# Backward of a memory-attention segment loop: order of the dS turns, the dK and dV products, and the row folds

## The chip, the cores and the metric

The kernel runs on one core of a Trainium2 chip. The metric is device time in microseconds (us) of one execution, from the first to the last instruction. Before the change it is 3257.82 us, the median of 3 runs (3256.99 to 3260.57).

## What is computed

The reference is one layer and its gradients: a layer norm with a modulation, an attention with recurrent memory, a second layer norm and a gated feed-forward part. The kernel returns the output and the gradients for x, the first memory, Wq, Wk, Wv, Wo, the three feed-forward weights, c and w_mod. What matters here is the attention and its gradient. The sequence of 2048 rows is cut into 64 segments of 32 rows; each segment has 8 memory rows in front, which are the first 8 output rows of the segment before it:

```python
mem = mem0
for s in range(n_seg):                      # 64 segments
    h = jnp.concatenate([mem, xs], axis=1)  # 8 + 32 rows
    q, k, v = (jnp.einsum('btd,dhe->bhte', h, W) for W in (Wq, Wk, Wv))   # 32 heads of 128
    scores = jnp.einsum('bhqe,bhke->bhqk', q, k) * scale
    p = _softmax(jnp.where(mask[None, None], scores, -1e9), axis=-1)
    o = jnp.einsum('bhqk,bhke->bhqe', p, v)
    o = jnp.einsum('bhte,hed->btd', o, Wo)
    mem = o[:, :M, :].copy()
    outs.append(o[:, M:, :])
```

The backward pass goes through the segments from the last to the first. The gradient of a segment's memory rows goes into the segment before it, so the 64 steps depend on each other.

## The kernel before, in words

The program has phases: the forward loop over segments (phase2), the feed-forward part with its gradients (phase3), the backward loop over segments (phase4) and the weight gradients (phase5). The change touches phase4 and two helpers which phase2 uses too.

**Tiling of a backward step.** The 32 heads of a segment are packed three to a group of 120 rows, 11 groups in all. The groups are handled in three parts of 4, 4 and 3 groups (`NP`, `PG`), because a PSUM tile holds 4 groups of 128 columns. A step of the loop at L1384 does this, in program order:

- `col_pass` (L1464) multiplies the incoming gradient by Wo; the two halves are copied out as `RAd`, one by VectorE and one by ScalarE. `turn` (L1469) transposes them into `dOT`.
- `dp`, `prod` and `ds` (L1472 to L1484) form dS: TensorE accumulates `dp_ps`, VectorE multiplies it by the stored probabilities (L1425).
- `grad_mm("dVT", ...)` gives dV in three parts (`gv0` to `gv2`), `grad_mm("dKT", ...)` gives dK (`gk0` to `gk2`) and `grad_part("dQT", ...)` gives dQ. Each part is a PSUM tile `g_ps` (L1436), which `grad_out` copies to SBUF through `evac` (L61 is ScalarE, L63 VectorE).
- dQ needs dS transposed. `dstt(pi)` (L1448) makes a part of it: TensorE transposes into a PSUM tile `tps` (L1352), and ScalarE copies that into `dST`.
- `dht` (L1455) multiplies dV, dK and dQ by the transposed weights, 96 narrow matmuls (L211) which accumulate in one PSUM tile, `dh_ps`. Four column groups of it have to be added up: `fold_split` (L271) writes a high and a low bf16 part of the tile (`dh_hi` by ScalarE, L278; `dh_lo` by VectorE, L282), and `fold_sum` (L286) adds the groups by matmuls with a selection matrix, into `dh_ft`. ScalarE copies the memory rows of that to `dyT_next` (L1523), with which the next step begins.
- `store_rows` (L295) casts `dh_ft` to bf16 on VectorE (`dh_tb`, L299) and appends a function to the list `self.later`. `pop_later` takes one function from that list and runs it: it transposes, copies (`dh_rb`, L305) and stores the rows from GpSimd (L306).

**The tail block.** The last 8 rows of each segment are collected over four segments (`TailRows`) and multiplied by the weights as one block, a quarter of its 96 matmuls per step (`chunk`), into a PSUM tile `dh_tps`. When the fourth quarter is done, `split` runs `fold_split` on that tile (`dh_b_hi`, `dh_b_lo`), and appends the sum (`dh_b_ft`) to `self.later`. Both uses of `fold_split` share their SBUF buffers by tag.

**What sets the order.** `pin` (L251) chains each engine's instructions of the loop in the order in which they are written. So the order of the calls in the loop is the order on every engine: an instruction that waits holds up all that stands behind it on its engine.

**PSUM.** `psp` has 6 buffers which all tiles with the tag "p" share in turn (`pass_ps`, `turn_ps`, `g_ps`, `dp_ps`, `tps`, `dh_ft` and so on), and `psb` has one each for `dh_ps` and `dh_tps`. A tile with the tag "p" can be written only when the tile six before it has been copied out.

**Transfers.** SyncE issues, in this order per step: the DMA transposes that turn dVT, dKT and dQT into rows (`rows_x`, L1444, three buffers in turn), the loads of `Qst` and `Kst` for the next step (L1357; one buffer each, so a load waits for the products that read the old content), and the loads of the stored forward tiles (L1340, L1343). GpSimd issues the stores of `rows_x` (L1446), by `store_rows_x`, in the next step, and small copies of tail rows into `dOst` (L1372).

Of the kernel before, what the change touches and what calls it, by code (L numbers as in the profile page):

```python
# [7 lines left out]
BF16 = mybir.dt.bfloat16  # L8
# [11 lines left out]
class Cfg:  # L20
    def __init__(self, NS=64, phases=("p0", "p1", "p2", "p3", "p4", "p5")):
        self.S_full = 2048
        self.D = 512
        self.DC = 4
        self.H = 32
        self.E = 128
        self.T = 32
        self.M = 8
        self.L = 40
        self.F = 1792  # L30
        self.FC = 14
        self.NS = NS
        self.S = NS * self.T
        self.NT = self.S // 128
        self.G = 11
        self.XW = 33 * 40 + 8
        self.scale = self.E ** -0.5
        self.phases = phases


class K:
# [226 lines left out]
                self.tc.add_manual_dep(ins, last[ins.engine].name, mybir.DependencyInfo(  # L268
                    mybir.DependencyClass.NoSync, mybir.DependencyReason.DATA), reason="program order")

    def fold_split(self, pool, ps, name):  # L271

        nc = self.nc
        parts = []
        for h in range(2):
            sl = slice(256 * h, 256 * h + 256)
            hi = pool.tile([128, 256], BF16, name=name + "_hi", tag=f"hi{h}", bufs=1)
            nc.scalar.activation(hi[:], ps[:, sl], AF.Copy)  # L278
            parts.append(hi)
        for h in range(2):  # L280
            lo = pool.tile([128, 256], BF16, name=name + "_lo", tag=f"lo{h}", bufs=1)
            nc.vector.tensor_tensor(lo[:], ps[:, 256 * h:256 * h + 256], parts[h][:], op=ALU.subtract)  # L282
            parts.append(lo)
        return parts
# [951 lines left out]
    def phase4(self):  # L1236
# [7 lines left out]
        with self.p4_ctx as ctx:  # L1244
            WqT, WkT, WvT, WoT, negones = self.WqT, self.WkT, self.WvT, self.WoT, self.negones
# [4 lines left out]
            sb2 = ctx.enter_context(tc.tile_pool(name="p4s2", bufs=2, reuse_waits="tile"))  # L1250
            psp = ctx.enter_context(tc.tile_pool(name="p4ps", bufs=6, space=PSUM, reuse_waits="tile"))
            psb = ctx.enter_context(tc.tile_pool(name="p4psb", bufs=1, space=PSUM, reuse_waits="tile"))
            NP = 3
# [28 lines left out]
            def part3(t, pi):  # L1282
                return t[:, pi * PW:min((pi + 1) * PW, G * GW)].rearrange("p (g x) -> p g x", x=GW)
# [71 lines left out]
            def load_rows(t, dram, s):  # L1355
                if s >= 0:
                    nc.sync.dma_start(gl3(t)[0:120, :, :], dram[s, 0:120, :, :])  # L1357
# [16 lines left out]
            dO_tails(NS - 1)  # L1374
            nseg_t = 128 // T
            row_stores = []

            def store_rows_x(left):
                while len(row_stores) > left:
                    row_stores.pop(0)()  # L1380
# [3 lines left out]
            for s in reversed(range(NS)):  # L1384
# [43 lines left out]
                def grad_part(nm, lh, rh, xt, pi, eng):  # L1428
                    grad_out(nm, xt, pi, eng, grad_mm(nm, lh, rh, pi))

                def grad_mm(nm, lh, rh, pi):
                    ps = ps_f32("g_ps")
                    n = min(PG, G - pi * PG)
                    for j in range(n):
                        g = pi * PG + j
                        nc.tensor.matmul(ps[:, j, :], lhsT=lh[:, g * GW:(g + 1) * GW], rhs=rh[:, g * GW:(g + 1) * GW],  # L1436
                                         start=True, stop=True)
                    return ps

                def grad_out(nm, xt, pi, eng, ps):  # L1440
                    self.evac(eng, part3(xt, pi), ps[:, 0:min(PG, G - pi * PG), :])
                    if pi == NP - 1:
                        rows = rxp.tile([128, G, 128], BF16, name="rows_x")
                        nc.sync.dma_start(rows[:], xt[:, :], transpose=True)  # L1444
                        dram = {"dVT": self.DVR, "dKT": self.DKR, "dQT": self.DQR}[nm][s]
                        row_stores.append(lambda: nc.gpsimd.dma_start(dram, rows[:]))  # L1446

                def dstt(pi):  # L1448
                    ps = transposes_part(dS, pi)
                    self.evac("act", part3(dST, pi), ps)  # L1450

                dh_ps = [None]
                n_dh = [0]
# [1 line left out]
                def dht(X, WT, pi):  # L1455
                    if dh_ps[0] is None:
                        dh_ps[0] = psb.tile([128, 512], F32, name="dh_ps", tag="dh")
                    for h in range(pi * PG * 3, min(H, (pi + 1) * PG * 3)):
                        off = (h // 3) * GW + (h % 3) * 32
                        self.col_mm(dh_ps[0], X[:, off:off + 32], WT[:, h, :], n_dh[0], 3 * H)  # L1460
                        n_dh[0] += 1

                for hf in range(2):
                    self.col_pass(psp, WoT, hf, lambda c: dyT[:, c, :], RAd, ("dve", "act")[hf])  # L1464
                    nc.gpsimd.tensor_copy(dOst[0:96, 512 * hf:512 * hf + 512], RAd[0:96, 512 * hf:512 * hf + 512])  # L1465
                store_rows_x(1)
                if s == 0:
                    self.p5_first()
# [23 lines left out]
                store_rows_x(0)  # L1492
                if s == 0:
                    self.p5_second()
                gv2 = grad_mm("dVT", dOst, Pst, 2)
                dstt(0)
                gk0 = grad_mm("dKT", Qst, dS, 0)
                dstt(1)
                gk1 = grad_mm("dKT", Qst, dS, 1)
                grad_out("dKT", dKT, 0, "dve", gk0)  # L1500
                grad_out("dVT", dVT, 2, "act", gv2)
                dstt(2)
                gk2 = grad_mm("dKT", Qst, dS, 2)
                load_rows(Qst_t, self.QST, s - 1)
                if s > 0:
                    dO_tails(s - 1)
                grad_out("dKT", dKT, 1, "dve", gk1)
                grad_out("dKT", dKT, 2, "dve", gk2)
                self.pop_later()
                for pi in range(NP):  # L1510
                    grad_part("dQT", Kst, dST, dQT, pi, "act")
                load_rows(Kst_t, self.KST, s - 1)
                dht(dVT, WvT, 2)
                for pi in range(NP):
                    dht(dKT, WkT, pi)
                for pi in range(NP):
                    dht(dQT, WqT, pi)
                parts = self.fold_split(sb2, dh_ps[0], "dh")
# [2 lines left out]
                ft = self.fold_sum(psp, parts, "dh", "p")  # L1521
                if dyT_next is not None:
                    nc.scalar.activation(dyT_next[:, :, 0:M], ft[:, :, 0:M], AF.Copy)  # L1523
                tail.split()
                if s > 3:
                    if s4 >= 2:
                        proj_b(s // 4 - 1, 3 - s4)()
# [2 lines left out]
                then = None  # L1530
# [4 lines left out]
                        for c in range(DC):  # L1535
                            nc.sync.dma_start(dm[:, c * 128:(c + 1) * 128], rb[32 * c:32 * c + M, :])

                self.store_rows(psp, sb2, ft, self.DHA[s], "dh", "p", then)
                if s4 == 0:
                    tail.begin(s, [WvT, WkT, WqT])  # L1540
            store_rows_x(0)
            self.pin(i0)
            tail.finish()
# [258 lines left out]
class TailRows:  # L1802

    def __init__(self, k, pool, psp, psb, n, name, dram_b, npieces=4):
        self.k, self.pool, self.psp, self.psb, self.n, self.name = k, pool, psp, psb, n, name
        self.dram_b, self.npieces = dram_b, npieces
        self.cur = None
        self.pieces = []  # L1810
        self.whole = None
# [10 lines left out]
    def begin(self, s0, ws):  # L1822
        while self.pieces:
            self.chunk()
        self.split()
        cfg, H = self.k.cfg, self.k.cfg.H
        tiles, self.cur = self.cur, None
        order = [(i, h) for i in range(self.n) for h in range(H)]
        per = len(order) // self.npieces
        st = {}  # L1830

        def piece(u):
            def f():
                if u == 0:
                    st["ps"] = self.psb.tile([128, 512], F32, name=f"{self.name}_tps", tag="b")
                for n in range(u * per, (u + 1) * per):
                    i, h = order[n]
                    self.k.col_mm(st["ps"], tiles[i][:, h, :], ws[i][:, h, :], n, len(order))
                if u == self.npieces - 1:
                    self.whole = st["ps"], s0  # L1840
            return f

        self.pieces = [piece(u) for u in range(self.npieces)]
# [4 lines left out]

    def split(self):
        if self.whole is None:  # L1850
            return
        (ps, s0), self.whole = self.whole, None
        parts = self.k.fold_split(self.pool, ps, self.name + "_b")

        def summed():
            ft = self.k.fold_sum(self.psp, parts, self.name + "_b", "p")
            self.k.store_rows(self.psp, self.pool, ft, self.dram_b[s0 // 4], self.name + "_b", "p")

        self.k.later.append(summed)

    def finish(self):
        while self.pieces:
            self.chunk()
        self.split()
        while self.k.later:
            self.k.pop_later()
# [85 lines left out]
```

## Time and profile before

The profile is of one execution of 3260.3 us. Busy times and shares are of the whole span.

| engine | busy us | share | instructions |
|---|---|---|---|
| TensorE (PE) | 3003.8 | 92% | 38650 |
| weight loads (PEld) | 1718.3 | 53% | 38650 |
| VectorE (DVE) | 1562.7 | 48% | 4106 |
| ScalarE (ACT) | 1225.3 | 38% | 2906 |
| GpSimd (POOL) | 1431.2 | 44% | 3037 |

The backward loop runs from about 1631 to 2655 us. In the stretch from 2000 to 2400 us TensorE is busy for 382.48 of 400 us, VectorE for 190.54, ScalarE for 187.11; the DMA engines move 257 GB/s.

In the rows of the views, L61 or L63 is a line of a helper, so a group is known by the tile that it writes and the tile that it reads (`dST<-tps`). "Idle before" gives how long the engine stood still ahead of an instruction, and what ended that. A busy TensorE isn't TensorE at its peak: matmuls overlap, and their ends are modelled. The chain of work follows the program back from its last instruction, at each step to what released it, so that it shows which of several waits ended last.

### The profile page before, as it was taken

What the parts mean: (1) busy time and instruction counts of PE and PEld (TensorE: products, weight loads), DVE (VectorE), ACT (ScalarE), POOL (GpSimd) and SP (SyncE); (2) the same over time, 40 slices, a digit from 0 to 9 for tenths busy, and PEclk for the clock granted to TensorE, in tenths of its full rate; (3) what the DMA queues carried; (4) which work ended last, traced back from release to release, by engine and by line L of the source; (5) the groups of instructions that cost most, each with busy time, mean ns of one, the idle gap of its engine ahead of it and who ended that gap; (6) DMA issues with size and microseconds to landing.
All of it is one profiled execution on the core that took longest, in us unless ns stands there. A gap on an engine that the chain in (4) does not pass through costs nothing.

```text
span 3260.3 us, 96121 instructions
## 1 busy us (share of the span) xinstructions
PE 3003.8 (92%) x38650; PEld 1718.3 (53%) x38650; DVE 1562.7 (48%) x4106; ACT 1225.3 (38%) x2906; POOL 1431.2 (44%) x3037
## 2 busy tenths in 40 slices
PE   6999999999998799988989999999999979999999
PEld 3555555555555444445555555555555544454454
DVE  5655655666655777633244444444444431322321
ACT  3555555555554333312144444444444420100111
POOL 3555555655555466520244444444444431333322
PEclk8999999999999899999999999999999999999999
DMA  8565555555566898897589999999999999998886
GB/s 295 175 172 169 172 170 167 169 166 171 169 165 181 212 216 214 204 270 227 187 223 251 252 253 257 259 258 265 254 256 245 252 238 219 240 209 191 198 229 162
DMA packets 862018, 699.40 MB, mean 215 GB/s; under 512 B 560690, under 2 KB 734274, under 8 KB 861444
## 3 DMA queue, kind: packets, MB, share of 16 engines
q1 hardware_dynamic: 737220, 483.44, 62.9%
q0 software_dynamic: 52912, 147.43, 13.2%
q10 hardware_dynamic: 71440, 62.40, 7.6%
q8 instruction: 304, 4.98, 0.7%
q14 instruction: 142, 1.16, 0.1%
HBM read 293.60 MB, written 275.02 MB: 174 GB/s over the span
## 4 chain that ended last, share of the span: by engine, by line
PE 43%; DMA 8%; ACT 2%; issue 2%; DVE 1%; POOL 1%; SPq 1%; ACTq 0%; DVEq 0%; POOLq 0%
PE dh_ps L211 10%; PE gps L1746 9%; PE pass_ps L222 4%; PE g_ps L1436 4%; PE gps5o L1759 3%; PE gps L1146 3%; PE dh_tps L211 3%; DMA rows<-DKR 2%; DMA Kst<-KST 2%; DMA rows<-OSR 1%; PE dp_ps L1415 1%; ACT RAd L61 1%; PE tps L1352 1%; PE dp_ps L1423 1%; PE dh_ft L291 1%
## 5 line engine op out<-in xcount | busy, mean ns | idle before, releaser
L1746 PE MATMUL gps<-rows,hrows 128*128 128x512 bf16 (+2 forms) x2160 | 419.5, 357 | 4.8 <-DVE ot L63 4.3
L1746 PEld LDWEIGHTS <-hrows 128*128 128x128 bf16 x2160 | 211.6, 98 | 211.0 <-issue 7.3
L222 PEld LDWEIGHTS <-hT 128*32 128x32 bf16 x6144 | 158.7, 97 | 177.5 <-ACT hT L785 24.5
L1465 POOL COPY dOst<-RAd 96x512 bf16<-96x512 bf16 x128 | 77.5, 612 | 376.1 <-DVE RAd L63 367.1
L282 DVE TENSOR_TENSOR dh_lo<-dh_ps,dh_hi 128x256 bf16<-128x256 f32 x128 | 48.4, 420 | 322.5 <-ACT dh_hi L278 322.5
L1750 POOL DMA_DIRECT2D out_dram<-ot x108 | 81.2, 754 | 235.5 <-DVE ot L63 141.1
L792 POOL TENSOR_TENSOR Pst<-Pst,rden 120x1408 bf16<-120x1408 bf16 x63 | 159.4, 2531 | 18.5 <-issue 7.7
L63 DVE CAST ot<-gps 128x512 bf16<-128x512 f32 (+3 forms) x76 | 47.8, 632 | 248.6 <-DMA out_dram<-ot 117.9
L1759 PE MATMUL gps5o<-WoT,rows 128*128 128x512 bf16 x600 | 131.8, 382 | 24.1 <-DMA rows<-OSR 24.1
L61 ACT ACTIVATE ot<-gps 128x512 bf16<-128x512 f32 (+3 forms) x75 | 41.1, 548 | 282.8 <-DMA out_dram<-ot 111.5
L306 POOL DMA_DIRECT2D AOA<-at_rb x64 | 36.7, 574 | 248.8 <-DVE at_rb L305 135.4
L61 ACT ACTIVATE dST<-tps 128x512 bf16<-128x512 bf16 (+1 forms) x192 | 102.2, 567 | 105.5 <-PE tps L1352 105.5
L222 PE MATMUL pass_ps<-Wv,hT 128*32 128x512 bf16 x2048 | 122.2, 381 | 18.0 <-ACT hT L785 18.0
L63 DVE CAST dKT<-g_ps 128x512 bf16<-128x512 f32 (+1 forms) x192 | 112.2, 640 | 50.3 <-issue 44.2
L694 DVE TENSOR_TENSOR Ost<-or_ps,rden 120x512 bf16<-120x512 f32 (+1 forms) x192 | 124.3, 647 | 23.1 <-PE or_ps L692 1.2
L211 PE MATMUL dh_ps<-WvT,dVT 128*32 128x512 bf16 x2048 | 134.9, 384 | 0.0
L1425 DVE SCALAR_TENSOR_TENSOR dS<-dp_ps,Pst_l 128x512 bf16<-128x512 f32 (+1 forms) x192 | 112.2, 640 | 32.2 <-PE dp_ps L1423 32.1
L222 PE MATMUL pass_ps<-WoT,dyT 128*32 128x512 bf16 x2048 | 122.5, 381 | 5.1 <-ACT dyT L1523 5.1
L211 PE MATMUL at_ps<-Wo,OT 128*32 128x512 bf16 x2048 | 122.3, 381 | 0.0
L211 PE MATMUL dh_ps<-WkT,dKT 128*32 128x512 bf16 x2048 | 121.7, 379 | 0.0
L211 PE MATMUL dh_ps<-WqT,dQT 128*32 128x512 bf16 x2048 | 121.7, 379 | 0.0
L222 PE MATMUL pass_ps<-Wk,hT 128*32 128x512 bf16 x2048 | 121.6, 379 | 0.0
(409 smaller groups left out, 7231.1 us busy)
## 6 DMA issues: line engine op xcount, KB each, us to landing
OSR<-Ost SPq DMA_DIRECT2D x64, 352.0 KB
OT<-OT SPq DMA_DIRECT2D x64, 352.0 KB
PS<-Pst SPq DMA_DIRECT2D x64, 352.0 KB
OT_l<-OT SPq DMA_DIRECT2D x64, 352.0 KB
Pst_l<-PS SPq DMA_DIRECT2D x64, 352.0 KB
DVR<-rows_x POOLq DMA_DIRECT2D x64, 352.0 KB, 5.5
DKR<-rows_x POOLq DMA_DIRECT2D x64, 352.0 KB, 7.2
DQR<-rows_x POOLq DMA_DIRECT2D x64, 352.0 KB, 5.4
```

Of the source, the lines that this page charges most:

```text
L61: return nc.scalar.activation(out, in_, AF.Copy)
L63: return nc.vector.tensor_copy(out, in_)
L211: self.nc.tensor.matmul(ps[32 * j:32 * j + 32, :], lhsT=lhsT, rhs=w, start=(n < 4), stop=(n >= total - 4), tile_position=(0, 32 * j))
L222: self.nc.tensor.matmul(ps[32 * j:32 * j + 32, :], lhsT=lhs(c), rhs=rhs, start=(c == 0), stop=(c == DC - 1), tile_position=(0, 32 * j))
L694: nc.vector.tensor_tensor(part3(Ost, pi)[0:120, 0:n, :], or_ps[0:120, 0:n, :], rden[:, pi * PG:pi * PG + n].unsqueeze(2).to_broadcast([120 ...
L792: nc.gpsimd.tensor_tensor(Pst[0:120, :, :], Pst[0:120, :, :], rden[:, :].unsqueeze(2).to_broadcast([120, G, 128]), op=ALU.mult)
L1146: nc.tensor.matmul(ps[:], lhsT=h2r[:, j, c * 128:(c + 1) * 128], rhs=xr[:, j, :], start=(j == 0), stop=(j == NT - 1))
L1425: nc.vector.scalar_tensor_tensor(out=part3(dS, pi), in0=ps[:, 0:n, :], scalar=cfg.scale, in1=part3(Pst, pi), op0=ALU.mult, op1=ALU.mult)
L1436: nc.tensor.matmul(ps[:, j, :], lhsT=lh[:, g * GW:(g + 1) * GW], rhs=rh[:, g * GW:(g + 1) * GW], start=True, stop=True)
L1746: nc.tensor.matmul(ps[:, 0:ng * E], lhsT=hrows[:, tp_, c * 128:(c + 1) * 128], rhs=rows[:, tp_, 0:ng * E], start=(tp_ == 0), stop=(tp_ == ...
L1750: nc.gpsimd.dma_start(outw[c * 128:(c + 1) * 128, h0:h0 + 3 * (ng - 1) + 1:3, :], ot[:, 0:ng * E].rearrange("p (h e) -> p h e", e=E))
L1759: nc.tensor.matmul(pss[gg][:], lhsT=rows[:, tp_, gg * E:(gg + 1) * E], rhs=dyrows[:, tp_, :], start=(tp_ == order[0]), stop=(tp_ == order[ ...
```

## The change

The loop body is put in another order, one copy goes to another engine, and two helpers run later.

- All three `dstt` (the turns of dS) stand ahead of the three dK products. The third dV product (`gv2`), which stood ahead of them all, goes behind dK. The aim is that dST is ready when dQ wants it.
- The copy of the middle part of dST is made by VectorE instead of ScalarE, and the copy-out of `gv2` stands behind both remaining ones on ScalarE.
- The load of `Qst` is issued ahead of the copies of dK, and dK's DMA transpose comes ahead of dV's.
- In `dht`, dK comes ahead of the third part of dV.
- The tail block's `split` moves from the end of the step in which its fourth quarter was computed into the next step, between dQ and `dht`; its sum is run by a `pop_later` after dK and dV of `dht`. `begin` doesn't split any more, `finish` does so first.
- `store_rows`, with its cast `dh_tb`, is put off to the next step, behind `col_pass`.
- `fold_split` and `TailRows` get a `tags` argument with the default "", which nothing sets.

```diff
                 def dstt(pi):
                     ps = transposes_part(dS, pi)
-                    self.evac("act", part3(dST, pi), ps)
+                    self.evac("dve" if pi == 1 else "act", part3(dST, pi), ps)
...
+                if pend:
+                    pend.pop()()
                 store_rows_x(1)
...
+                for pi in range(NP):
+                    dstt(pi)
+                gks = [grad_mm("dKT", Qst, dS, pi) for pi in range(NP)]
+                load_rows(Qst_t, self.QST, s - 1)
                 gv2 = grad_mm("dVT", dOst, Pst, 2)
-                dstt(0)
-                gk0 = grad_mm("dKT", Qst, dS, 0)
-                dstt(1)
-                gk1 = grad_mm("dKT", Qst, dS, 1)
-                grad_out("dKT", dKT, 0, "dve", gk0)
-                grad_out("dVT", dVT, 2, "act", gv2)
-                dstt(2)
-                gk2 = grad_mm("dKT", Qst, dS, 2)
-                load_rows(Qst_t, self.QST, s - 1)
                 if s > 0:
                     dO_tails(s - 1)
-                grad_out("dKT", dKT, 1, "dve", gk1)
-                grad_out("dKT", dKT, 2, "dve", gk2)
+                for pi in range(NP):
+                    grad_out("dKT", dKT, pi, "dve", gks[pi])
+                grad_out("dVT", dVT, 2, "act", gv2)
                 self.pop_later()
                 for pi in range(NP):
                     grad_part("dQT", Kst, dST, dQT, pi, "act")
+                split = tail.split()
                 load_rows(Kst_t, self.KST, s - 1)
-                dht(dVT, WvT, 2)
                 for pi in range(NP):
                     dht(dKT, WkT, pi)
+                dht(dVT, WvT, 2)
+                if split:
+                    self.pop_later()
                 for pi in range(NP):
                     dht(dQT, WqT, pi)
                 parts = self.fold_split(sb2, dh_ps[0], "dh")
...
-                tail.split()
...
-                self.store_rows(psp, sb2, ft, self.DHA[s], "dh", "p", then)
+                pend.append(lambda ft=ft, s=s, then=then: self.store_rows(psp, sb2, ft, self.DHA[s], "dh", "p", then))
                 if s4 == 0:
                     tail.begin(s, [WvT, WkT, WqT])
+            pend.pop()()
             store_rows_x(0)
...
     def begin(self, s0, ws):
         while self.pieces:
             self.chunk()
-        self.split()
...
     def split(self):
         if self.whole is None:
-            return
+            return False
...
     def finish(self):
+        self.split()
         while self.pieces:
             self.chunk()
         self.split()
```

More of the change, by code (lines that the diff above doesn't have):

```diff
@@ L269, in pin_behind, with fold_split @@
                     mybir.DependencyClass.NoSync, mybir.DependencyReason.DATA), reason="program order")
-    def fold_split(self, pool, ps, name):
+    def fold_split(self, pool, ps, name, tags=""):
         nc = self.nc
@@ L276, in fold_split @@
             sl = slice(256 * h, 256 * h + 256)
-            hi = pool.tile([128, 256], BF16, name=name + "_hi", tag=f"hi{h}", bufs=1)
+            hi = pool.tile([128, 256], BF16, name=name + "_hi", tag=f"{tags}hi{h}", bufs=1)
             nc.scalar.activation(hi[:], ps[:, sl], AF.Copy)
@@ L280, in fold_split @@
         for h in range(2):
-            lo = pool.tile([128, 256], BF16, name=name + "_lo", tag=f"lo{h}", bufs=1)
+            lo = pool.tile([128, 256], BF16, name=name + "_lo", tag=f"{tags}lo{h}", bufs=1)
             nc.vector.tensor_tensor(lo[:], ps[:, 256 * h:256 * h + 256], parts[h][:], op=ALU.subtract)
@@ L1376, in phase4 @@
             row_stores = []
+            pend = []
             def store_rows_x(left):
@@ L1802, with __init__ @@
 class TailRows:
-    def __init__(self, k, pool, psp, psb, n, name, dram_b, npieces=4):
+    def __init__(self, k, pool, psp, psb, n, name, dram_b, npieces=4, tags=""):
         self.k, self.pool, self.psp, self.psb, self.n, self.name = k, pool, psp, psb, n, name
-        self.dram_b, self.npieces = dram_b, npieces
+        self.dram_b, self.npieces, self.tags = dram_b, npieces, tags
         self.cur = None
@@ L1850, in split @@
         if self.whole is None:
-            return
+            return False
         (ps, s0), self.whole = self.whole, None
-        parts = self.k.fold_split(self.pool, ps, self.name + "_b")
+        parts = self.k.fold_split(self.pool, ps, self.name + "_b", self.tags)
         def summed():
@@ L1859, in split @@
         self.k.later.append(summed)
+        return True
     def finish(self):
+        self.split()
         while self.pieces:
```

## The prediction, written before the changed kernel was run

> **What bounds the kernel now.** I read the page, then the stretches of the span, because the change is confined to the backward loop over segments, about 1631 to 2655 us. All times below are us.
>
> The stretches of that loop, columns: window, length, busy time and instruction count of PE, weight loads, DVE, ACT, POOL, then granted clock, DMA share and GB/s:
>
> ```profile
> 1660.00:2640.00 980.00, 923.37 (x15322) 555.14 (x15319) 460.05 (x1252) 453.58 (x1165) 434.65 (x1077) 1.00 1.11 254
> ```
>
> TensorE is busy 94% of it, every other compute engine under half, and the DMA share is over 1. So TensorE's order sets the pace and the DMA system is nearly full beside it. 62 steps between two like points (the dVT turns issued at 1645.66 and 2631.85) average 15.91; twelve of them without a wait for a transfer, from 2014.61 to 2200.97, average 15.53.
>
> Then the chain of work in order of time for one step (start, us, what), from the last dV product to the big product:
>
> ```profile
> 2198.84 0.28 PE g_ps L1436 x3
> ...
> 2200.18 0.62 PE g_ps L1436 x7
> 2200.80 0.03 ACTq L61
> 2200.83 0.08 ACT dVT L61
> 2200.91 0.39 ACT dST L61
> 2201.30 0.04 issue
> 2201.34 0.33 PE g_ps L1436 x3
> 2201.67 4.00 PE dh_ps L211 x72
> ```
>
> 2201.67 - 2198.84 = 2.83 for 36 matmuls; at 4.00/72 = 0.056 each they need 2.0. The rest is one wait: the third dQ product needs the third part of dST. Why it is late is in the timeline of ScalarE:
>
> ```profile
> 2199.44 1.08 ACT L61 ACTIVATE dST<-tps 128x512 bf16<-128x512 bf16 x2 [1.60 <-PE tps L1352]
> 2200.41 0.50 ACT L61 ACTIVATE dVT<-g_ps 128x384 bf16<-128x384 f32 x1
> 2200.78 0.51 ACT L61 ACTIVATE dST<-tps 128x384 bf16<-128x384 bf16 x1
> ```
>
> The last dST copy stands behind two others and a dVT copy on one engine. The waits of TensorE over the loop (us, times, longest):
>
> ```profile
> PE g_ps L1436 <- ACT dST L61: 10.6, 32, 0.3
> PE g_ps L1436 <- DMA Kst<-KST: 10.2, 9, 2.1
> ```
>
> The first understates the loss (a modelled busy tail covers part of each gap). The second says that Kst sometimes lands too late for dQ. Its place in the queue, from SyncE's timeline:
>
> ```profile
> 2200.97 2.81 SPq L1444 DMA_TRANSPOSE rows_x<-dVT  x1
> 2203.88 0.90 SPq L1357 DMA_DIRECT2D Qst<-QST  x1
> 2204.91 1.70 SPq L1444 DMA_TRANSPOSE rows_x<-dKT  x1
> 2206.72 3.43 SPq L1444 DMA_TRANSPOSE rows_x<-dQT  x1
> 2210.59 0.34 SPq L1357 DMA_DIRECT2D Kst<-KST  x1
> ```
>
> Kst is issued 9.6 after the first turn; the next dQ starts at 2216.05, 5.5 after the issue. The chain's Kst waits show 5.5 to 6.4 from issue to landing where TensorE waited. So the slack is near zero in such steps.
>
> **What the Trainium skill says.** "PSUM — Partial Sum Buffer", Specifications: 8 banks per partition. The pools fill them (6 rotating, 2 accumulators), so a product waits for the copy-out of the tile six before it; no wait here is named so by the trace of before, but it decides the new order. The same page, "PSUM bank collisions raise a hardware error": two engines must not read one bank at once. The trace agrees: the dh_lo subtraction starts 0.69 after dh_hi (2205.72 to 2206.41), when both ScalarE copies (0.66) are over. "DMA: Bandwidth & Descriptors", "Issuing engines are not separate DMA queues": all queues share 16 DMA engines; the share of 1.11 with SyncE and GpSimd issuing fits.
>
> **The change, part by part.** One PSUM copy moves to another engine; no matmul and no transfer is added.
>
> 1. *Turns first, middle dS^T on VectorE.* The price is in the groups by shape:
>
> ```profile
> L63 DVE COPY btd<-turn_ps 128x512 bf16<-128x512 bf16 x15 | 6.4, 425 | 12.9 <-PE turn_ps L231 12.9
> L63 DVE CAST dKT<-g_ps 128x512 bf16<-128x512 f32 x126 | 81.2, 686 | 48.3 <-issue 44.2 <-POOL dyb L1185 2.4 <-POOL dOT L65 1.6
> ```
>
> The first row is the same copy on the same engine: 0.425. It stands ahead of the dKT casts. Replay of the step above from 2198.84: turns issue until 2199.45, dK until 2200.06, dV part 2 until 2200.23. Turn 1 ends at 2199.45 (issued 2199.06, four take 0.39), the copy starts 0.1 later as ScalarE's did, ends at 2199.98; the first dKT cast ends at 2200.67, all three (1.75 in the timeline) at 2201.7. ScalarE starts dST 0 at about 2199.3 and ends dST 2 at about 2200.3, so both are ready. dQ 0 and 1 issue until 2200.68. dQ 2 reuses the PSUM tile of dK 0 and starts after its cast, 2200.73, ending at 2200.90. The big product starts at 2200.90 instead of 2201.67: **0.77 saved**. dS itself is no new wait: its three DVE products end by 2198.78, and turn 2 is issued at 2199.29.
>
> 2. *dht of dKT before dVT part 2.* The casts end at 2200.67, 2201.3, 2201.7; the product reaches those parts (12 matmuls of 0.056 each) at 2200.90, 2201.57, 2202.2. Just in time: 0. dVT part 2, now copied last, has until 2202.7: 0.
>
> 3. *Cast of the fold rows (dh_tb, 0.28) behind the RAd copy.* VectorE idles 0.49 between RAd and its next copy (timeline at 2210.32), so it is hidden there. It came out of a place where it delayed RAd by 0.35 once in four steps (RAd at 2209.15, product over at 2208.8), but the transposes then wait for ScalarE's half anyway (2210.42): 0 both ways.
>
> 4. *Tail split moved into the next step, once in four (15 times).* ScalarE and VectorE idle 3 and 5 before dh_hi, so the copies cost nothing there. But the fold sum now follows within the same step. dQT copies end about 2202.3, then dh_b_hi, and by the 2206 pattern (hi at 2205.72, sum from 2206.89 to 2207.47) the sum runs from 1.17 to 1.75 after hi starts: 2203.4 to 2204.0. TensorE arrives at 2203.1, after 40 more matmuls. Queued behind the waiting sum are the dQ part of the product, then everything else. Cost 0.8 inline, where before it took 0.19 behind dS. In that step 4.37 (2212.77 to 2217.14) becomes 0.06 + 1.41 + 2.06 + 0.8 = 4.33: gain 0.
>
> 5. *Step after it (15 times).* A second row store falls before dQ and shifts the PSUM rotation by one, so dQ 2 waits for the second dKT cast (2201.3). 4.29 (2228.81 to 2233.10) becomes 0.06 + 1.41 + 2.66: 0.16 saved.
>
> 6. *SyncE.* Qst moves ahead of the turns, to about 2200.2, where SyncE is idle; about 1.0 leaves the stretch between first turn and Kst. But the first turn is now dKT's: it waits for the third cast, 2201.7 instead of 2200.97. Kst is thus issued at about 2210.4, as before, while its use comes earlier.
>
> Sum: 34 x 0.77 + 15 x 0.16 + 15 x 0 = 28.6. Against that, part 6: where Kst has no slack (about 15 of 64 steps, around 1790-1910 and 2470-2590) a stall at dQ does not delay the next dKT cast, so period and stall share the shortfall. With T = first turn to Kst landing = 9.4 + 5.6 and the cast 1.4 after an unstalled dQ, 2P = 15.1 + 16.4, P = 15.75 against 16.06 before: 0.3 per step instead of 0.45. I take off 4 for these steps in all. 3257.8 - 28.6 + 4 = **3233**.
>
> **Rivals.**
> - *DMA takes over everywhere.* For: share 1.11, Kst just in time. Against: only 11 of 64 steps show a Kst wait. Every step at 15.75 instead of 15.91 gives 64 x 0.16 = 10: 3248.
> - *More than forecast.* Turns back to back with no load between them, and Qst moved into SyncE's idle time, free the DMA queue; the Kst waits (10.2 on PE, 13.6 on weight loads) vanish too: about 3216.
> - *Slower.* The later first turn pushes the transfers into the state of the worst stretch: nine steps from 2405.25 to 2551.06 took 16.2 each. 64 x 0.29 = 19 more: 3276. For: the turn waits 0.7 more. Against: Qst leaves the chain.
>
> **How the numbers follow.** Forecast 0.57, full DMA bound 0.18, more than forecast 0.13, slower 0.12. The bounds of the unknowns: dST on VectorE costs 0.425 to 0.69 (its f32 cast), the latter delaying dQ 2 by 0.26 in 34 steps, 9 us; the fold-sum stall is 0.3 to 1.5, 7 us either way. Low 3214 takes in the case above forecast; high 3258 covers the DMA bound and part of the slower case. Faster by over 0.2% (below 3251.3): forecast, more, and two thirds of the DMA case, 0.80; same 0.11; slower 0.09.
>
> **What would show it.** ScalarE's dST wait gone from TensorE's list; the chain from the dV rows to the big product about 2.05 instead of 2.83 in ordinary steps; a new wait of dh_b_ft on dh_b_lo, 15 times; Kst waits not more than about 25. It would be wrong if Kst waits appear in most steps, or if dKT casts are named ahead of the big product.

## The result, and the profile after

The changed kernel takes 3233.1 us, the median of 4 runs (3227.67 to 3235.58), against 3259.2 us for the kernel before (4 runs, 3256.99 to 3263.17). The ratio is 0.9916, with a 95% interval of 0.9899 to 0.9934: 26 us, or 0.8%, faster. Measured a second time beside other kernels (e1 below), the ratio was 0.9911 (0.9894 to 0.9929). One of the six executions of e11 lasted 3879.78 us at a granted clock of 0.749, where all others had 0.98 to 0.99, and is left out of that kernel's numbers.

The profiled execution lasts 3233.1 us. The view of the backward loop in one window, columns as in the prediction (window, length, busy time of PE, weight loads, DVE, ACT, POOL, granted clock, DMA share, GB/s):

```profile
1660.00:2620.00 960.00, 915.74 (x15440) 552.01 (x15435) 492.79 (x1332) 433.66 (x1114) 439.87 (x1083) 1.00 1.12 262
```

TensorE is busy 95% of the window instead of 94%, VectorE 51% instead of 47% (it has taken over a copy), and the transfers run at 262 GB/s instead of 254: the same bytes per step, in shorter steps.

The chain of work of an ordinary step, from the first parts of dV in the big product to the rest of it:

```profile
2231.30 1.41 PE dh_ps L211 x24
2232.71 0.72 PE tps L1352 x11
2233.43 1.40 PE g_ps L1437 x25
2234.83 4.00 PE dh_ps L211 x72
```

No ScalarE piece stands between TensorE's any more. 36 matmuls now take 2.12 us, where it was 2.83. The copies, from the timeline of the same step:

```profile
2233.14 0.98 ACT L61 ACTIVATE dST<-tps 128x512 bf16<-128x512 bf16 x2 [1.43 <-PE tps L1352]
...
2233.30 0.42 DVE L63 COPY dST<-tps 128x512 bf16<-128x512 bf16 x1 [0.53 <-PE tps L1352]
...
2233.75 1.75 DVE L63 CAST dKT<-g_ps 128x512 bf16<-128x512 f32 x3
...
2234.31 0.49 ACT L61 ACTIVATE dVT<-g_ps 128x384 bf16<-128x384 f32 x1 [0.20 <-PE g_ps L1437]
```

Both engines copy parts of dST at the same time, and the dV copy comes last. TensorE's list of waits over the loop has lost the line for dST. Of the lines that answer to those shown before, the one for Kst is left; the third line is of the weight loads and shows the moved fold sum (us, times, longest):

```profile
PE g_ps L1437 <- DMA Kst<-KST: 1.2, 2, 0.6
PE dh_b_ft L291 <- DVE dh_b_lo L282: 1.3, 3, 0.7
PEld L291 <- ACT dh_b_hi L278: 6.4, 15, 0.4
```

SyncE's order, from its timeline. The Qst load is issued early, and the three transposes follow each other:

```profile
2218.53 0.34 SPq L1357 DMA_DIRECT2D Qst<-QST  x1
2220.09 3.12 SPq L1445 DMA_TRANSPOSE rows_x<-dKT  x1
2223.31 2.87 SPq L1445 DMA_TRANSPOSE rows_x<-dVT  x1
2226.29 2.55 SPq L1445 DMA_TRANSPOSE rows_x<-dQT  x1
2228.93 0.54 SPq L1357 DMA_DIRECT2D Kst<-KST  x1
```

From the first transpose to Kst it is 8.8 us, where it was 9.6.

**A measure for the rest of this text.** The steps repeat in a pattern of four, so I took from each trace the starts of the second pair of RAd transposes, and from them the length of each step. The *regular* length is the median over the steps of one kind; the *excess* is what the 59 intervals behind the first four took beyond the regular lengths of their kinds, in sum. "Tail step" is the step that carries the tail block's sum after the change, "next step" the one behind it, which carries a second row store. The excess can fall below zero, since two of the last steps are 0.5 shorter than the regular ones in almost every trace. In us:

| kernel | tail step | next step | ordinary, third | ordinary, fourth | mean of the four | excess |
|---|---|---|---|---|---|---|
| before | 15.98 | 15.96 | 15.55 | 15.46 | 15.74 | 8.8 |
| after | 16.07 | 15.49 | 14.85 | 14.75 | 15.29 | 9.7 |

So an ordinary step gained 0.705, the next step 0.475, and the tail step lost 0.095. (15.74 - 15.29) x 63 steps = 28 us of the 29.4 that the loop gained: from the first to the last of these transposes it went from 1010.2 to 980.8 us.

### The profile page after: what moved, and what is told of

Its sections match the earlier page's. It is cut to its first block, busy times and chain, and to the rows that moved or that the text cites. A ratio compares the mean times of both kernels' runs of the same rounds, so it can differ in the third digit from the quotient of the medians.

```text
span 3233.1 us, 96019 instructions
## 1 busy us (share of the span) xinstructions
PE 2984.2 (92%) x38574; PEld 1709.9 (53%) x38650; DVE 1589.7 (49%) x4170; ACT 1200.4 (37%) x2842; POOL 1430.5 (44%) x3037
## 4 chain that ended last, share of the span: by engine, by line
PE 43%; DMA 8%; ACT 2%; issue 2%; DVE 1%; SPq 1%; POOL 1%; ACTq 0%; DVEq 0%; POOLq 0%
PE dh_ps L211 9%; PE gps L1748 9%; PE pass_ps L222 4%; PE g_ps L1437 4%; PE gps L1146 3%; PE gps5o L1761 3%; PE dh_tps L211 2%; DMA rows<-DKR 2%; PE tps L1352 2%; PE dp_ps L1416 1%; DMA rows<-OSR 1%; PE dp_ps L1424 1%; ACT RAd L61 1%; PE dh_ft L291 1%; PE turn_ps L1318 1%
## 5 line engine op out<-in xcount | busy, mean ns | idle before, releaser
L222 PE MATMUL pass_ps<-Wq,hT 128*32 128x512 bf16 x2048 | 121.6, 379 | 0.0
L61 ACT ACTIVATE dVT<-g_ps 128x512 bf16<-128x512 f32 (+1 forms) x192 | 107.8, 562 | 35.9 <-PE g_ps L1437 20.0
```

The source lines that it names most:

```text
L61: return nc.scalar.activation(out, in_, AF.Copy)
L222: self.nc.tensor.matmul(ps[32 * j:32 * j + 32, :], lhsT=lhs(c), rhs=rhs, start=(c == 0), stop=(c == DC - 1), tile_position=(0, 32 * j))
```

## The experiments

Each kernel was timed against the kernel before, next to others of the same group.

### Does the gain need the tail's move? (e1 to e4)

**e1, the changed kernel once more**, with no edit.

> The changed kernel once more, as the yardstick for the three kernels run beside it. Its ratio to the kernel before was 0.9916 (0.9899 to 0.9934): every theory expects the same again, about 0.992.

Measured: 0.9911 (0.9894 to 0.9929), 3231.93 us. Regular 15.29, excess 9.2, as in the first trace.

**e2, only the new order and the copy on VectorE.** The early load of Qst belongs to it; tail split and row cast are where they were:

```diff
-                    self.evac("act", part3(dST, pi), ps)
+                    self.evac("dve" if pi == 1 else "act", part3(dST, pi), ps)
 ...
-                gv2 = grad_mm("dVT", dOst, Pst, 2)
-                dstt(0)
-                gk0 = grad_mm("dKT", Qst, dS, 0)
 ...
+                for pi in range(NP):
+                    dstt(pi)
+                gks = [grad_mm("dKT", Qst, dS, pi) for pi in range(NP)]
+                load_rows(Qst_t, self.QST, s - 1)
+                gv2 = grad_mm("dVT", dOst, Pst, 2)
 ...
-                dht(dVT, WvT, 2)
                 for pi in range(NP):
                     dht(dKT, WkT, pi)
+                dht(dVT, WvT, 2)
```

> The kernel before with only the new order around dS, dK, dQ and dht, and the middle dS^T copy on VectorE; tail split and row cast stay where they were. Theory: the whole gain is the removed dST wait (0.705 us in 34 steps, 0.475 in the 15 steps that carry a second row store), and the moved tail split costs what the tail step doesn't show. Without the move the tail step keeps its 0.475 as well: 34 x 0.705 + 30 x 0.475 = 38, some of which transfers take back, so about 3224 us or ratio 0.989, 5 to 12 us faster than the full change. Rival: the tail move is needed, since the split at the end of the step delays RAd or the PSUM tiles run out: ratio 0.992 or above, not faster than the full change.

Measured: 0.9906 (0.9887 to 0.9925), 3229.02 us. The order together with the copy on VectorE gives the whole gain. It was expected to be faster than the full change, which the times can't tell. The steps can: the tail step is 15.62 instead of 16.07, the next step 15.61 instead of 15.49, the fourth 14.82 instead of 14.75, mean 15.22 instead of 15.29. So the moved split costs 0.45 in one step and gives 0.12 and 0.07 back in others.

**e3, only the tail's move:**

```diff
                     grad_part("dQT", Kst, dST, dQT, pi, "act")
+                split = tail.split()
                 load_rows(Kst_t, self.KST, s - 1)
                 dht(dVT, WvT, 2)
                 for pi in range(NP):
                     dht(dKT, WkT, pi)
+                if split:
+                    self.pop_later()
 ...
-                tail.split()
 ...
```

> The kernel before with only the tail split moved into the next step, between dQ and dht, and its sum run behind dK and dV of dht. Theory: the sum now waits on TensorE for dh_b_lo in 15 steps. In the old order TensorE comes to it later (2203.9 us in the step of the prediction) and the copies are ready at 2203.8 to 2204.35, so 0.5 us inline instead of 0.19: 15 x 0.3 = 4.6 us slower, ratio 1.0014. Rival: it frees VectorE ahead of RAd and is worth up to 15 x 0.2 = 3 us: ratio 0.999.

Measured: 1.0018 (1.0008 to 1.0028), 3265.92 us. It is slower, by the amount expected. The tail step grew from 15.98 to 16.43, the next step shrank from 15.96 to 15.84: 15 x (0.45 - 0.12) = 5 us, the same 0.45 and 0.12 as in e2.

**e4, the full change with the tail's sum one place later**, behind the dQ part of the big product:

```diff
-                if split:
-                    self.pop_later()
                 for pi in range(NP):
                     dht(dQT, WqT, pi)
+                if split:
+                    self.pop_later()
```

> The full change with the tail block's sum run one place later, behind the dQ part of dht, where its operands have long been ready. Theory: the 0.8 us inline in 15 steps becomes 0.2 to 0.3 (8 small matmuls, and a start of dh_hi delayed by them, since the tail's halves share their buffers): 15 x 0.5 = 7.5 us faster than the full change, ratio 0.9893. Rival: the buffers' hand-over to dh_hi puts the wait behind dht instead, where nothing covers it: same as the full change, or slower.

Measured: 0.9889 (0.9869 to 0.9909), 3223.22 us, 8.7 us less than e1 beside it. The two intervals overlap, so the times alone don't prove it, but the tail step fell from 16.07 to 15.46 with all other kinds unchanged: 15 x 0.61 = 9 us. The chain of a tail step of the changed kernel shows what was removed:

```profile
2203.61 0.99 ACT dQT L61 x2
2204.60 0.56 ACT dh_b_hi L278 x2
...
2205.19 0.77 DVE dh_b_lo L282 x2
...
2206.00 0.24 PE dh_b_ft L291 x3
2206.24 1.84 PE dh_ps L211 x32
```

From the dQ copies to the sum the chain runs over ScalarE and VectorE. TensorE meanwhile does 40 matmuls of the big product, comes to the sum at 2205.47, and waits inside it for both parts of dh_b_lo. And in e4:

```profile
2194.16 4.00 PE dh_ps L211 x72
2198.16 0.30 PE dh_b_ft L291 x8
2198.45 1.41 PE dh_tps L211 x24
2199.86 0.30 PE dh_ft L291 x8
```

The 32 dQ matmuls cover the wait. The hand-over of the shared buffers to dh_hi, feared by the rival, shows no cost: the tail's own quarter and the fold sum of the step behind it take 1.41 + 0.30 = 1.71 us here, and 1.80 in the chain of the changed kernel (2208.08 to 2209.88).

### Which part of the reordering matters? (e5, e7, e8, e9)

**e5, the full change with all dST copies on ScalarE:**

```diff
-                    self.evac("dve" if pi == 1 else "act", part3(dST, pi), ps)
+                    self.evac("act", part3(dST, pi), ps)
```

> The full change with all three dS^T copies on ScalarE again. Theory: the order alone isn't enough, the third copy on one engine ends 0.49 us later (ScalarE starts these copies 0.49 apart) and dQ 2 waits about 0.2 us in each of 64 steps, and the dQ copies and with them dh_b_hi come 0.24 later in the 15 tail steps: about 16 us slower than the full change, ratio to the kernel before 0.996. The wait of g_ps for dST is back on TensorE's list. Rival: the order did it all, since in the new order no dV copy stands between the dST copies any more: ratio 0.991 to 0.992.

Measured: 0.9936 (0.9914 to 0.9959), 3242.65 us. The chain of an ordinary step has a wait for a dST copy again:

```profile
2233.78 0.74 PE tps L1352 x11
...
2234.70 0.60 ACT dST L61
2235.30 0.04 issue
2235.35 0.93 PE g_ps L1437 x11
```

It isn't the wait that was expected (dQ 2, 0.2). The first dQ product needs only the first part of dST, which was ready at 2234.8, and starts 0.05 after the copy of the second has ended (2235.30); the second dQ product starts at 2235.73, 0.05 after the copy of the third (2235.68). So each waits for a part that it doesn't read, about 0.4 in all. That fits the six shared PSUM buffers: counted back in the order of writing, these are the tiles that the second and third turn wrote. Ordinary steps take 15.23 and 15.13: of the 0.705, the second engine is worth 0.38 once the order is new, and the order by itself 0.33. The second engine in the old order wasn't run. The mean of the four is 15.59, 0.30 above the changed kernel, which would be 19 us. In the profile and in the times only 6 to 8 us of that are seen, because the excess has gone from 9.7 to -1.2. So the regular steps grew by about the amount expected, and something beside them did not; e11 looks at that.

**e7, only the row cast put off:**

```diff
+                if pend:
+                    pend.pop()()
                 store_rows_x(1)
 ...
-                self.store_rows(psp, sb2, ft, self.DHA[s], "dh", "p", then)
+                pend.append(lambda ft=ft, s=s, then=then: self.store_rows(psp, sb2, ft, self.DHA[s], "dh", "p", then))
 ...
+            pend.pop()()
             store_rows_x(0)
```

> The kernel before with only the row store (cast dh_tb) put off behind the next step's col_pass. Theory: VectorE has 0.49 us idle there for a cast of 0.28, and TensorE waits for ScalarE's half of RAd anyway: ratio 1.000, same within the interval. Rival: taking it from in front of RAd is worth 0.2 us a step once in four, ratio 0.999; or it delays the copies into dOT by up to 0.1 us a step, ratio 1.002.

Measured: 0.9995 (0.9978 to 1.0012). All four kinds of step are within 0.01 us of the kernel before. This part does nothing by itself.

**e8, e4 with the third dV product between the second and the third turn** (the edit against e4):

```diff
-                for pi in range(NP):
-                    dstt(pi)
+                dstt(0)
+                dstt(1)
+                gv2 = grad_mm("dVT", dOst, Pst, 2)
+                dstt(2)
```

> The kernel with the sum behind dQ (e4) and the third dV product put between the second and third turn of dS. After the change TensorE waits about 0.1 us in each step for the third part of dS ahead of the third turn; three matmuls of dV (0.17 us) fit there. Theory: that wait is work that could be covered, 64 x 0.1 = 6 us faster than e4, ratio 0.987. Rival: the PSUM tile of dV, copied out last on ScalarE, now stands in the rotation ahead of dQ and dQ waits for it: ratio 0.989 or above.

Measured: 0.9890 (0.9866 to 0.9914), not told apart from e4 by its time. Its regular steps are longer, 14.97 and 14.87 instead of 14.85 and 14.75. In a step of its trace the last dQ product starts 5.78 us from the step's second transposes, and the dV copy ends at 5.73: the rival's wait. What the expectation took from the list of weight loads, a wait of 0.1 for dS, isn't idle time of the matmuls: in e4 the turns start 3.81 after those transposes, right behind the 24 matmuls which take 1.41 from 2.40 on, and the third part of dS, which only the third turn needs, is ready at 3.81 too.

**e9, e4 with the old order in the big product, and e10, e4 once more beside it** (the edit of e9 against e4):

```diff
+                dht(dVT, WvT, 2)
                 for pi in range(NP):
                     dht(dKT, WkT, pi)
-                dht(dVT, WvT, 2)
```

> The kernel with the sum behind dQ (e4), and in dht the third part of dV ahead of dK again, as before the change. The prediction put this reordering at nothing, since the dK casts are ready just in time. In the trace of e4 dht begins at 5.92 us from the step's second transposes, and the copy of the third dV part ends at 5.97. Theory: with dV first, dht waits 0.1 us in each step, 64 x 0.1 = 6 us: ratio 0.991, so the reordering is part of the gain. Rival: the first dK cast is over only 0.3 us earlier and TensorE's later waits swallow it: ratio 0.989 as e4.

> e4 once more on another day's chip, as the yardstick for the run beside it and to see whether it beats the changed kernel: ratio 0.989, the changed kernel had 0.9916 and 0.9911.

Measured: e9 0.9900 (0.9881 to 0.9919), e10 0.9897 (0.9878 to 0.9916). The times don't tell them apart. The regular steps do, a little: 14.94 and 14.84 in e9, 14.85 and 14.75 in e4 and e10, as theory had it. The mean over the four kinds is 15.21 in e9, 15.14 in e4 and 15.15 in e10, so 0.06 to 0.07, or 4 us over the loop. e10 has an excess of 19.3 where e4 had 10.6, so one kernel's excess moves by 9 us from one trace to another.

### Do the transfers take something back? (e6, e11, e12)

**e6, the full change with the Qst load behind dK's transpose again:**

```diff
-                load_rows(Qst_t, self.QST, s - 1)
                 gv2 = grad_mm("dVT", dOst, Pst, 2)
 ...
                     grad_out("dKT", dKT, pi, "dve", gks[pi])
+                load_rows(Qst_t, self.QST, s - 1)
```

> The full change with the load of Qst issued behind dK's DMA transpose, so between two transposes as in the kernel before. Theory of the prediction (the transfers are nearly full, and taking the load out from between the transposes is what let TensorE run faster without waiting for Kst): Kst waits of 10 to 15 us come back, ratio 0.994 to 0.996. Rival: the place of that load doesn't matter, transfers had room: ratio as the full change, 0.991 to 0.992, Kst waits under 5 us.

Measured: 0.9912 (0.9889 to 0.9935), 3236.2 us, Kst waits of 4.3 us on TensorE, regular 15.29, excess 11.7. The place of that load has no effect that can be seen at this pace.

**e11, the full change with one load per step less:**

```diff
-            loads = {}
+            loads, vts = {}, {}
 ...
-                    d["VT"] = ldp.tile([128, cfg.XW], BF16, name="VT_l")
-                    nc.sync.dma_start(d["VT"][:], self.VT[s])
+                    if s >= NS - 2:
+                        vts[s % 2] = ldp.tile([128, cfg.XW], BF16, name="VT_l")
+                        nc.sync.dma_start(vts[s % 2][:], self.VT[s])
+                    d["VT"] = vts[s % 2]
```

> The full change with the load of VT (332 KB, some 8% of a step's transfers) left out in all but the first two backward steps, so that those read an old VT: that part of the computation is wrong, instructions of the five engines are unchanged. Theory: in the changed kernel single steps are longer than the regular ones of their kind, together about 10 us in the 59 steps behind the first, and that is what the transfers take back. With fewer of them these go: regular steps 15.29 as before, excess under 3 us, about 8 us faster than the full change, ratio 0.989. Rival: the excess has another cause: ratio 0.991 to 0.992, excess near 10.

Measured: 0.9880 (0.9854 to 0.9905), 3219.77 us. Regular steps 15.29, to the hundredth those of the changed kernel; the excess is 1.5. The same window of e1 and of e11, first e1:

```profile
1660.00:2600.00 940.00, 896.70 (x15123) 538.85 (x15120) 481.57 (x1303) 424.86 (x1092) 428.75 (x1060) 1.00 1.13 262
```

```profile
1660.00:2600.00 940.00, 902.09 (x15260) 543.45 (x15256) 483.94 (x1308) 425.98 (x1098) 430.58 (x1069) 1.00 1.07 242
```

With the same instructions on the engines, fewer transfers (242 instead of 262 GB/s) let more of them through in the same time. This points to the transfers as the cause of the excess, some 8 us in the changed kernel. It is one trace, though, and the two intervals of the times overlap; e10 shows how far one kernel's excess can move, so the size is not settled. Nor does the edit tell the bytes of a load from its place in SyncE's queue, since it takes both away.

The traces name the transfers more directly. Here are TensorE's waits in the longest step of the changed kernel (19.92 us, 4.43 more than its kind), and in the longest of e1 (18.96, 4.22 more), which has two:

```profile
1904.88 0.59 PE L1437 MATMUL g_ps<-Pst_l,dOst 128*128 128x128 bf16 x4 [3.07 <-DMA dOst<-RBd]
```

```profile
2178.20 0.38 PE L1437 MATMUL g_ps<-Pst_l,dOst 128*128 128x128 bf16 x4 [1.20 <-DMA dOst<-RBd]
2186.03 0.79 PE L1437 MATMUL g_ps<-dST,Kst 128*128 128x128 bf16 x11 [2.73 <-DMA Kst<-KST]
```

The first wait of each is for the small copies of tail rows into dOst which GpSimd issues, a transfer that neither the prediction nor an experiment took into account. The longest steps of the kernel before, e7, e9 and e12 also wait for one of these two transfers or for both. Why a copy comes late in one step and not in the others isn't shown.

**e12, e5 and e6 together:**

```diff
-                    self.evac("dve" if pi == 1 else "act", part3(dST, pi), ps)
+                    self.evac("act", part3(dST, pi), ps)
 ...
-                load_rows(Qst_t, self.QST, s - 1)
                 gv2 = grad_mm("dVT", dOst, Pst, 2)
 ...
+                load_rows(Qst_t, self.QST, s - 1)
```

> e5 (all dS^T copies on ScalarE, regular steps of 15.59 and no excess) with the Qst load back between the transposes as in e6. Theory of the prediction: with the load between the transposes the transfers need more time per step, as the kernel before shows an excess of 8.8 at steps of 15.74: excess 5 to 10 us, ratio 0.996. Rival: the load's place has no weight, the excess depends only on how fast TensorE asks: excess about 0, ratio 0.9936 as e5.

Measured: 0.9943 (0.9925 to 0.9961), regular 15.59, excess 6.7. The interval holds e5's value, and most of the excess comes from one step of 21.7 us, in which TensorE waits 1.68 for dOst and 2.72 for Kst. It settles nothing: whether the load's place matters at this pace stays open.

## Why the prediction was right

It said 3233 us (3214 to 3258); 3233.1 was measured. The mechanism is the one named: the wait for the third part of dST is gone, and that is the gain. That the figure fits to the microsecond is luck. The prediction had the loop gain 24.6; the two traces show 29.4, and the times 26.1. Its sum started from 3257.8 for the kernel before, for which the median of four runs is 3259.2. In the trace of the changed kernel the rest of the program took 2.2 us more than before, which the trace of e1 doesn't repeat.

- *Turns first, middle dS^T on VectorE (part 1):* right. 0.77 was worked out, 0.705 came. The part was 2.06 long by the prediction and is 2.12; the VectorE copy took the 0.425 that was taken for it. e2 shows that this order, with that of the big product, is the whole gain, and e5 that order and second engine are each about half of it.
- *dht order (part 2), put at 0:* against e4's order, e9 shows 0.1 in an ordinary step, about 4 us over the loop, and this 0.1 is contained in the 0.705 above. dK's casts are in time as predicted, but dV's copy, last on ScalarE, would not have been: in e4 it ends 5.97 after the step's second transposes, and the product begins at 5.92. The prediction priced only what the new order waits for, and not what the old one would have waited for there.
- *Row cast (part 3), put at 0:* right (e7).
- *Tail split (part 4):* the inline cost of 0.8 with its cause was right. In the trace TensorE starts the dQ part at 2206.17, about 0.75 after the 40 matmuls in front of the sum (from 2203.20 on, 0.056 each). For the tail step the sum was gain 0, measured -0.095. Both sizes behind this 0 were too large: with the tail left in place the new order gains 0.36 in this step (e2), where the sum would give about 0.7, and the move costs 0.45 in it, where the sum had 0.8 for 0.19. Why isn't shown. e3 shows the move by itself to be a loss and e4 that it can be had without one.
- *The step after it (part 5), put at 0.16:* wrong, 0.475 came. The step that failed is "dQ 2 waits for the second dKT cast". From the timelines of such a step, in order the second cast, the dV copy on ScalarE, and the dQ products 1 and 2:

```profile
2218.81 0.68 DVE L63 CAST dKT<-g_ps 128x512 bf16<-128x512 f32 x1
2218.70 0.49 ACT L61 ACTIVATE dVT<-g_ps 128x384 bf16<-128x384 f32 x1 [0.19 <-PE g_ps L1437]
2218.95 0.38 PE L1437 MATMUL g_ps<-dST,Kst 128*128 128x128 bf16 x4
2219.25 0.33 PE L1437 MATMUL g_ps<-dST,Kst 128*128 128x128 bf16 x3
```

dQ 1 starts 0.05 after the first cast (ended 2218.89), a wait of 0.16. dQ 2 starts at 2219.25, before the second cast ends (2219.49) and 0.05 after the dV copy has ended (2219.20), a wait of 0.08. Together they are the 0.23 by which this step gains less than an ordinary one; the prediction had 0.6. The PSUM tiles were counted by hand, six back in the order of writing. The waits in e5 and that of dQ 1 fit this count, that of dQ 2 doesn't, so the rule as the description of the kernel gives it doesn't hold for every tile; which tile dQ 2 took over is inferred from these times only. Worth 15 x 0.3 = 5 us more than predicted; the 0.065 x 34 = 2 us of part 1 and the 15 x 0.095 = 1.4 us of part 4 go the other way.
- *Transfers (part 6), 4 us taken off for Kst:* not seen. The excess went from 8.8 to 9.7, and the waits for Kst fell from 10.2 to 1.2 us. The prediction read the Kst waits of the kernel before as a mark of its order. Two other kernels in the old order, e3 and e7, show 1.8 and 1.5, so that they vary from trace to trace. Nor does the Qst load's place matter in the changed kernel (e6). What the runs speak for is that late transfers lengthen single steps, and not only those of Kst.

Of the rivals, "slower" and "DMA takes over everywhere" are refuted by the times. Of "more than forecast" one half came true, as the Kst waits of that trace nearly vanished, but the excess stayed (9.7), 3.1 of it in one wait for dOst, and the time stayed at the forecast. Nothing shows that the move of Qst did it: e6 has it back, and its Kst waits are 4.3, where e1 shows 4.1.

e4 is faster than the kernel before, and by its steps and its medians than the changed one too: 0.9889 and 0.9897 in two measurements, where the changed kernel had 0.9916 and 0.9911, with intervals that overlap. It differs from the changed kernel in the place of the two lines that run the tail block's sum.

## What to carry to other kernels

Look for the copy that ends last ahead of a matmul and count what stands before it on its engine: here putting the three producers together, ahead of copies that are wanted later, took away about one half of the wait, and giving one copy to an engine with idle time the other. Count the buffers too: by their times, the products in e5 waited for a buffer to come free, and not for their data. A piece of side work that hid behind something must be given a new place of the same kind when it moves; here the move by itself lost 5 us by its steps (e3), and two lines further on, behind 32 matmuls, it lost nothing (e4). Where late transfers stretch single steps, compare regular steps and not only totals: one kernel's excess moved by 9 us between two traces, a third of what the change is worth. Then ask of the longest steps which transfer they wait for.

## What the runs showed of the hardware that was not expected

- The excess doesn't follow the pace. With a regular step of 15.59 us it was -1.2 (e5) and 6.7 (e12), at 15.29 it was 9 to 12 (first trace, e1, e6), at 15.14 to 15.15 it was 10.6 and 19.3 (e4, e10), and kernels with 15.74 to 15.82 showed 8.8, 3.9 and 3.6 (before, e7, e3). Single steps are stretched, by amounts which differ between traces of one kernel. In the longest of them TensorE waits up to 3.1 us for the small copies into dOst (the changed kernel, e9) and up to 3.4 us for Kst (e9). The first step of the loop, which the measure leaves out, waits 6.1 to 7.0 us for these copies in every trace. With fewer loads (e11, one trace) the excess was 1.5.
- The weight loads' list put 24.6 us on dS in the changed kernel, 58 times, while in the steps looked at (e4) the matmuls behind those loads follow the ones ahead of them without a gap. So a wait of weight loads isn't one of the matmuls.
